# A fused channel-attention and SwiGLU kernel on one core: x's parts rounded in other steps, and a fourth pair's and a softmax's work placed elsewhere

## The chip, the cores and the metric

The kernel runs on one core of one Trainium2 chip. The metric is the device time of one execution in microseconds (us); lower is better. PE is TensorE (PEld its weight loads), DVE is VectorE, ACT is ScalarE, POOL is GpSimd, SP is SyncE, which here issues DMAs.

## The reference

```python
B, N, C, DFF = 2, 6016, 256, 1536
qn = q / (norm(q, axis=1) + 1e-6)           # over the N rows
kn = k / (norm(k, axis=1) + 1e-6)
s = kn.transpose(0, 2, 1) @ qn / tau        # C x C for each batch element
a = softmax(s)                              # exp(s - max), divided by its sum
x = (v @ a).reshape(B * N, C)               # 12032 rows
xn = x / sqrt(mean(x * x, -1) + 1e-6) * rms_g
g, val = xn @ w_gate, xn @ w_val
out = (silu(g) * val) @ w_out
```

## The kernel before

All matmuls run on operands split in a high and a low part: the high part is the value rounded to the matmul's type (a copy on ACT), the low part is the value minus its high part (a subtraction on POOL or DVE). Each product is then three matmuls, high by high, high by low and low by high.

A first phase reads q and k and builds batch element 0's attention. The rest runs over 24 blocks (`NB`) of up to 512 rows, block j = 0 to 23; blocks 0 to 11 (`B1` = 12) belong to batch element 0, the others to element 1. Every block is worked off in 12 steps f (`NF`), one per 128 columns of the hidden layer. Blocks 2 to 22 use a Strassen-like scheme for gate and value: `emit_step` emits seven products per step (each three matmuls) over three steps in flight. In one step PE does product 7 and 2 of the step two back (its sums are taken by DVE at L808 and L809), 3 and 6 of the step one back (ACT copies at L815), 5 and 1 of the new one (ACT copies at L820), then the output matmuls that are due, then product 4 of the oldest, which writes a PSUM buffer that DVE must have read at L808. Product 5 takes the PSUM buffer that was freed by the last reader of the step before: DVE at L836 after an odd step, ACT at L842 after an even one.

Two steps make one pair p of the hidden layer. In an odd step DVE multiplies gate and value (L827, L836) and ACT rounds the result (`gx`, `gy`, `gz` at L739) with POOL taking the low parts (L747). From block 4 on (`STRA`) the output product uses the seven-product scheme for pairs 1 to 4, which needs `run_turned` in the following even step on DVE: L726, L727 and L731. Its constants, sums of the weights `w_out`, are built by `build_so(k, piece)`: piece 0 sums on DVE (L659, L669), piece 1 rounds on ACT (L677), piece 2 takes low parts on DVE (L679). k = 3 is the fourth pair.

While block j goes through the steps, the next blocks are prepared by small pieces hung into its steps. The order of these pieces is written out by hand in tables: `steady` holds for j >= 5 and says what is emitted at the end of step f, `steady_mid` what is emitted inside step f, ahead of its output matmuls; `turn4` and `turn4_mid` are the tables of block 4. `at(j, f, ...)` adds single pieces at the end of step f of block j. Each engine works through its own instructions strictly in this order.

For block n = j + 1 the pieces are: the transposed rows `xnT` come back by 16 DMAs on SP's queue; ACT scales them (L558); POOL makes differences (`xp`, L570 and L575); then x is rounded in two rounds. Round 0 (`xh0` on ACT at L601 from `xnT`, `xl0` on POOL at L613) and round 1 (`xh1` on ACT at L601 from `xp`, two instructions of 128x512; `xl1`, two subtractions of 128x512 at L613) fill the buffers `xt` that block n's products read. For n = j + 2 there are the parts of v (`vh0`, `vl0`, `vh1`, `vl1`; L443 on ACT, L448 on POOL), x itself (L459 on PE), its squares (L475), its scaling (`n0`, `n1`; L500). Block 22 rounds its successor in another way and has no round 1. For j - 1 there are the output's sums (`copy` L1018, `sums_` L1028, `c0` and `c1` L1037) and the store (L1048).

`turn4` takes over step 1's `xh0` from `steady` and has `xh0` again in step 3. Batch element 1's softmax is spread over blocks 3 to 9: `softmax_exp` (L300, ACT) and `softmax_div` (L315 to L320, DVE: four instructions for each of the two halves, c = 0 and 1). Its result is first used for block 12, by the product x in step 3 of block 10.

Of the kernel before, what the change touches and what calls it, by code (L numbers as in the profile page):

```python
# [19 lines left out]
def kernel(  # L20
# [17 lines left out]
    nc = tc.nc  # L38
# [10 lines left out]
    STRA = 4  # L49
# [248 lines left out]
    def softmax_exp(b, c):  # L298
        z, mx = sm_t[b]
        nc.scalar.activation(  # L300
            out=z[:, c, :], in_=z[:, c, :], func=AF.Exp, scale=-1.0, bias=mx[:, c:c + 1],
            accum_out=mx[:, KC + c:KC + c + 1],
        )

    def softmax_div(b, c):
        if c == 0:
            a_hl[b] = []
            for i in range(2):
                a_hl[b].append(sm_p.tile([P, KC, C], F32R, tag=f"a{i}", name=f"a{i}_{b}"))
                if b == i == 0:  # L310
                    sm_p.tile([P, 8], F32, tag="apart", name="apart")
        ah, al = a_hl[b]
        z, mx = sm_t[b]
        s = mx[:, KC + c:KC + c + 1]
        nc.vector.tensor_scalar(out=s, in0=s, scalar1=1e-9, scalar2=None, op0=ALU.add)  # L315
        nc.vector.reciprocal(s, s)
        nc.vector.tensor_scalar(
            out=ah[:, c, :], in0=z[:, c, :], scalar1=s, scalar2=None, op0=ALU.mult
        )
        nc.vector.scalar_tensor_tensor(  # L320
            out=al[:, c, :], in0=z[:, c, :], scalar=s, in1=f32(ah[:, c, :]),
            op0=ALU.mult, op1=ALU.subtract,
        )
# [16 lines left out]
    B1 = NB // B  # L340
# [262 lines left out]
    def emit_xT_low(j, i, engine=nc.gpsimd):  # L603
        if j == NB - 1:
            if i == 0:
                engine.tensor_tensor(
                    out=xT[j][1], in0=moved[j][:, :, :blocks[j][2] * P], in1=f32(xT[j][0]),
                    op=ALU.subtract,
                )
            return  # L610
        src, hi, lo = xT_round(j, i)
        for o, x, y in zip(lo, src, hi):
            engine.tensor_tensor(out=o, in0=x, in1=f32(y), op=ALU.subtract)  # L613
# [41 lines left out]
    def build_so(k, piece):  # L655
        p = PAIRS[k]
        if piece == 0:
            t = s_tmp["so", k] = pool["wk"].tile([P, 4, 2 * P], F32, tag="wk", name=f"wo_{k}")
            nc.vector.tensor_tensor(  # L659
                out=t[:, :2], in0=f32(wo[0][:, 2 * p:2 * p + 2]), in1=f32(wo[1][:, 2 * p:2 * p + 2]),  # L660
                op=ALU.add,
            )
            a12, a22, a11, a21 = (t[:, i, e * P:(e + 1) * P] for i in range(2) for e in range(2))
            s1, s2, s3, s4 = (t[:, 2 + i, e * P:(e + 1) * P] for i in range(2) for e in range(2))
            for o, i0, i1, op in (
                (s1, a21, a22, ALU.add), (s2, s1, a11, ALU.subtract),
                (s3, a11, a21, ALU.subtract), (s4, a12, s2, ALU.subtract),
            ):
                nc.vector.tensor_tensor(out=o, in0=i0, in1=i1, op=op)  # L669
        else:  # L670
            t = s_tmp["so", k][:, 2:].rearrange("p i n -> p (i n)")
            src = (t[:, :3 * P], t[:, 3 * P:])
            hi, lo = (x[k] + [w[:, 2 * p + 1, P:]] for x, w in zip(so_hl, wo))
            if len(hi) > len(src):
                src = (t[:, :2 * P], t[:, 2 * P:3 * P], t[:, 3 * P:])
            for o, x in zip(hi, src) if piece == 1 else ():
                nc.scalar.activation(out=o, in_=x, func=AF.Copy)  # L677
            for o, x, y in zip(lo, src, hi) if piece == 2 else ():
                nc.vector.tensor_tensor(out=o, in0=x, in1=f32(y), op=ALU.subtract)  # L679
# [381 lines left out]
    with tc.manual_schedule():  # L1061
# [133 lines left out]
        def at(j, f, go):  # L1195
            extra.setdefault((j, f), []).append(go)
# [73 lines left out]
        at(STRA - 1, 6, new_so)  # L1270
        for i, k, f in ((0, 0, 10), (1, 0, 11), (2, 0, 12), (0, 1, 12), (1, 1, 13), (2, 1, 14), (0, 2, 14), (1, 2, 15)):
            at(STRA - 1 + f // NF, f % NF, lambda k=k, i=i: build_so(k, i))
        at(STRA, 7, last_so)
        for i in range(3):
            at(STRA, 9 + i, lambda i=i: build_so(3, i))

        at(3, 1, lambda: inverse_norms(1))
        at(3, 2, lambda: spread_norms(1, ps_m, "m"))
        at(3, 3, lambda: keep_norms(1))
        at(3, 5, lambda: softmax_min(1, 0))  # L1280
        at(3, 6, lambda: softmax_min(1, 1))
        at(7, 4, lambda: (softmax_exp(1, 0), softmax_exp(1, 1)))
        at(B1 - 3, 9, lambda: softmax_div(1, 0))
        at(B1 - 3, 11, lambda: softmax_div(1, 1))

        steps = [(j, f) for j in range(NB) for f in range(NF)]
        owed = []
# [30 lines left out]
        def of(m, go):  # L1318

            def run(j):  # L1320
                n = j + m
                if m < 0 and n < WINO or n >= NB:
                    return
                go(n)
            return run
# [11 lines left out]
        vh0, vl0, vh1, vl1 = (of(2, lambda n, go=go, h=h: go(n, h)) for h in range(2) for go in (split_v_high, split_v_low))  # L1337
        xh0, xl0, xh1, xl1 = (of(1, lambda n, go=go, i=i: go(n, i)) for i in range(2) for go in (emit_xT_high, emit_xT_low))

        steady = {  # L1340
            0: (vl0,),
            1: (xh0,),
            2: (copy, sums_),
            3: (vh1,),
            4: (xh1, c0, c1),
            5: (xl1, n0),
            6: (m0,),
            7: (load,),
            8: (m1,),
# [3 lines left out]
            1: (scale,),  # L1353
            2: (parts, v1),
            3: (xl0, x0),
            4: (vl1, q0, r0),
            5: (x1, q1, r1, store),
            6: (n1,),
            11: after(3, lambda n: split_v_high(n, 0)),
# [1 line left out]
        turn4 = {  # L1361
            **steady,
            0: (vh0, vl0),
            2: (),
            3: (xh0, v1),
            4: (vh1, c0, c1),
# [70 lines left out]
        for i, (j, f) in enumerate(steps):  # L1437
            outs = []
            owed.append((i + (2 if j < WINO else LAG + (j == NB - 1)), j, f))
            while owed and owed[0][0] <= i:  # L1440
                outs.append(owed.pop(0)[1:])
            k = min(j, 5)
            hooks = [
                [lambda go=go: go(j) for go in table[k].get(f, ())] for table in (pres, mids, ends)
            ]
            if j < WINO or j == NB - 1:
                if j == NB - 1 and f < 2:
                    low = []
                    emit_step(
                        None, None, i % 2, outs, mid=[lambda: low.append(emit_hidden(j, f, (), False))]  # L1450
                    )
                    low.pop()()
                    outs = []
                else:
                    if j == NB - 1 and f == 2:
                        run_later()
                    emit_hidden(j, f, weights.get((j, f), ()))
                for go in hooks[1]:
                    go()
                for o in outs:  # L1460
                    emit_all(o)
            else:
                if j == WINO and f < 2:
                    for o in outs:
                        emit_all(o)
                    outs = []
                emit_step(j, f, i % 2, outs, *hooks[:2])
                while late:
                    late.pop(0)()
            for go in hooks[2]:  # L1470
                go()
            for go in extra.get((j, f), []):
                go()
# [37 lines left out]
```

## Time and profile before

| | before |
|---|---|
| median of three runs | 1268.98 us (1267.22 to 1269.09) |
| profiled execution, its own time | 1268.32 us |
| its span, first to last instruction | 1266.5 us |
| mean granted TensorE clock | 0.999 |
| busy share PE / DVE / ACT / POOL | 99 / 79 / 68 / 53 % |

The span is that of the profiled execution; the 1.8 us between it and the execution's own time lie outside the first and the last instruction. A busy share is the time in which an engine had an instruction running. Matmuls overlap, so PE counts as busy through short gaps between them.

### The profile page before, as it was taken

How to read it: one execution, taken by the hardware profiler on the slowest of the kernel's cores; microseconds unless marked ns; L12 is line 12 of the kernel's file. 1: busy time of each engine (PE TensorE's matmuls, PEld its weight loads, DVE VectorE, ACT ScalarE, POOL GpSimd, SP SyncE). 2: the span in 40 equal slices, each digit the busy share in tenths (PEclk: the TensorE clock that was granted, in tenths of full speed). 3: DMA queues.
4: the chain of work that ended last, by engine and by line, in shares of the span. 5: the costliest groups of instructions: out<-in, count | busy, mean ns of one | idle time of the engine just before them, and what ended most of it. 6: DMA issues, size and time to landing. Idle time of an engine off the chain costs nothing.

```text
span 1266.5 us, 25188 instructions
## 1 busy us (share of the span) xinstructions
PE 1251.8 (99%) x9312; PEld 1198.9 (95%) x9312; DVE 1004.8 (79%) x1637; ACT 859.7 (68%) x1767; POOL 671.8 (53%) x564
## 2 busy tenths in 40 slices
PE   9999999999999999999999999999999999999998
PEld 8898989998999999999999999999999999999998
DVE  5789698666978878878879779779779779788773
ACT  5666547666677787777677677676777767777652
POOL 0120356574675566574675665665665765755430
PEclk9999999999999999999999999999999999999999
DMA  9868312020220211211202202202202202101211
GB/s 309 316 223 263 111 34 49 20 34 18 51 34 19 50 25 28 45 24 34 41 18 45 38 15 51 35 18 51 35 18 51 35 18 51 30 19 30 48 37 30
DMA packets 229371, 75.97 MB, mean 60 GB/s; under 512 B 186880, under 2 KB 220800, under 8 KB 229248
## 3 DMA queue, kind: packets, MB, share of 16 engines
q1 hardware_dynamic: 228416, 73.12, 24.3%
q8 instruction: 73, 1.20, 0.4%
q10 hardware_dynamic: 832, 1.25, 0.3%
q14 instruction: 50, 0.41, 0.1%
HBM read 48.50 MB, written 14.42 MB: 50 GB/s over the span
## 4 chain that ended last, share of the span: by engine, by line
PE 87%; DVE 4%; DMA 3%; ACT 2%; SPq 1%; issue 1%; POOL 1%; ACTq 0%; DVEq 0%; POOLq 0%
PE pu L779 39%; PE po L1003 23%; PE pq L779 6%; PE px L459 5%; PE s L185 5%; PE pg L896 3%; PE pv L896 3%; PE po L949 3%; DMA raw<-in_k_dram 2%; SPq L548 1%; SPq L353 0%; DVE gx L726 0%; DVE zg L808 0%; POOL gz L747 0%; DVE zg L727 0%
## 5 line engine op out<-in xcount | busy, mean ns | idle before, releaser
L779 PE MATMUL pu<-xt,w 128*128 128x256 f32 x2268 | 391.9, 281 | 1.6 <-DVE zg L808 1.3
L779 PE MATMUL pu<-xt,s 128*128 128x256 f32 x2268 | 355.5, 282 | 4.5 <-ACT t L815 2.8
L747 POOL TENSOR_TENSOR gy<-zg,gy 128x512 fp32r<-128x512 f32 x126 | 176.9, 1404 | 313.9 <-ACT gy L739 294.3
L779 PEld LDWEIGHTS pu<-xt,w 128*128 128x128 f32 x2268 | 326.5, 188 | 13.0 <-DVE zg L808 2.1
L779 PEld LDWEIGHTS pu<-xt,s 128*128 128x128 f32 x2268 | 311.7, 189 | 17.0 <-DVE zg L836 3.6
L820 ACT ACTIVATE t<-pu 128x512 f32<-128x512 f32 x252 | 151.5, 601 | 105.6 <-DVE zv L809 55.0
L1003 PE MATMUL po<-gx,w 128*128 128x256 f32 (+1 forms) x984 | 190.6, 314 | 0.0
L827 DVE TENSOR_TENSOR zg<-zg,zv 128x768 f32<-128x768 f32 x126 | 169.2, 1343 | 11.3 <-DVE zv L809 0.5
L739 ACT ACTIVATE gx<-zg 128x768 fp32r<-128x768 f32 (+1 forms) x126 | 95.7, 760 | 113.9 <-DVE zg L836 65.9
L1003 PEld LDWEIGHTS po<-gx,w 128*128 128x128 f32 x984 | 140.9, 189 | 4.7
L779 PE MATMUL pq<-xt,w 128*128 128x256 f32 x756 | 130.0, 280 | 0.0
L815 ACT ACTIVATE t<-pu 128x256 f32<-128x256 f32 x252 | 95.5, 379 | 45.0 <-PE pu L779 44.7
L808 DVE TENSOR_TENSOR zg<-pu,t 128x512 f32<-128x512 f32 x126 | 86.1, 683 | 41.2 <-PE pu L779 23.8
L747 POOL TENSOR_TENSOR gz<-zg,gz 128x512 fp32r<-128x512 f32 x76 | 116.4, 1532 | 0.0
L779 PEld LDWEIGHTS pq<-xt,w 128*128 128x128 f32 x756 | 107.0, 189 | 0.0
L824 ACT ACTIVATE zg<-zg 128x768 f32<-128x768 f32 x126 | 105.6, 838 | 0.0
L808 DVE TENSOR_TENSOR zv<-pu,t 128x512 f32<-128x512 f32 x126 | 84.6, 672 | 16.4 <-ACT zg L842 7.6
L185 PE MATMUL s<-raw 128*128 128x256 f32 x376 | 85.9, 382 | 3.7 <-DMA raw<-in_k_dram 3.7
L747 POOL TENSOR_TENSOR gx<-zg,gx 128x512 fp32r<-128x512 f32 x50 | 65.2, 1304 | 41.1 <-ACT gx L739 40.9
L1003 PE MATMUL po<-gy,w 128*128 128x512 f32 x300 | 85.4, 393 | 0.0
L185 PEld LDWEIGHTS s<-raw 128*128 128x128 f32 x376 | 70.2, 191 | 14.4 <-DMA raw<-in_k_dram 3.2
L739 ACT ACTIVATE gy<-zg 128x512 fp32r<-128x512 f32 x126 | 79.9, 634 | 1.4 <-PE po L1003 1.1
(173 smaller groups left out, 2317.4 us busy)
## 6 DMA issues: line engine op xcount, KB each, us to landing
v<-in_v_dram SPq DMA_DIRECT2D x84, 128.0 KB, 3.7
xnT<-xw SPq DMA_DIRECT2D x336, 32.0 KB, 1.9
out_dram<-ob SPq DMA_DIRECT2D x84, 128.0 KB, 3.3
raw<-in_q_dram SPq DMA_DIRECT2D x20, 512.0 KB, 4.9
raw<-in_k_dram SPq DMA_DIRECT2D x19, 512.0 KB, 5.7
wraw<-in_moe_w_gate_dram SPq DMA_DIRECT2D x12, 256.0 KB, 5.7
wraw<-in_moe_w_val_dram SPq DMA_DIRECT2D x12, 256.0 KB, 6.4
wraw<-in_moe_w_out_dram SPq DMA_DIRECT2D x12, 256.0 KB, 6.5
```

The costliest lines, as they stand in the source:

```text
L185: nc.tensor.matmul(out=s_ps[b][:, c, :], lhsT=r[:, 1, t, c * P:(c + 1) * P], rhs=r[:, 0, t, :], start=(t0 + t == 0 and c == 0), stop=(t0 + ...
L459: nc.tensor.matmul(out=px[:, i, :], lhsT=w[:, c, i * P:(i + 1) * P], rhs=x[:, c, :], start=(i == 0 and c == 0 and m == 0), stop=(c == KC - ...
L739: nc.scalar.activation(out=gh, in_=hh, func=AF.Copy)
L747: engine.tensor_tensor(out=gl, in0=hh, in1=f32(gh), op=ALU.subtract)
L779: nc.tensor.matmul(out=out, lhsT=wm[wi], rhs=xm[xi], start=(start and q == 0), stop=(q == 2), skip_group_check=True,)
L808: nc.vector.tensor_tensor(out=z[:, 1:], in0=u, in1=t[:, :2], op=ALU.add)
L815: nc.scalar.activation(out=mt[:, 0], in_=mu[:, 1], func=AF.Copy)
L820: nc.scalar.activation(out=nt[:, 1:], in_=nu, func=AF.Copy)
L824: nc.scalar.activation(out=zg[:, 1:], in_=zg[:, 1:], func=AF.Silu)
L827: nc.vector.tensor_tensor(out=zg[:, 1:], in0=zg[:, 1:], in1=z, op=ALU.mult)
L896: nc.tensor.matmul(out=t[:, :n], lhsT=wgv[wi][:, f, c, wj, :], rhs=x[xi][:, c, :n], start=(m == 0), stop=(m == 3 * KC - 1),)
L1003: nc.tensor.matmul(out=acc[b][:, o:o + g.shape[-1]], lhsT=w, rhs=g, start=first, stop=True, skip_group_check=True,)
```

## The change

Four things change, and all are places in the order; the arithmetic stays, but for one thing that was done twice.

- In blocks 5 to 22 `xh1` moves from the end of step 4 to the end of step 3, behind `vh1`. `xl1` moves from POOL at the end of step 5 to DVE inside step 4 (`xl1v`).
- In block 4 the first of the two `xh0` is taken out.
- The fourth pair's constants are built in steps 5, 6 and 9 of block 4, not in steps 9, 10 and 11.
- The two halves of `softmax_exp` are done after step 8 of block 7 and after step 8 of block 8, not both after step 4 of block 7. The two halves of `softmax_div` are done after step 1 and inside step 2 of block 10, not after steps 9 and 11 of block 9.

```diff
--- before.py
+++ after.py
@@ -1270,18 +1270,19 @@
         at(STRA - 1, 6, new_so)
         for i, k, f in ((0, 0, 10), (1, 0, 11), (2, 0, 12), (0, 1, 12), (1, 1, 13), (2, 1, 14), (0, 2, 14), (1, 2, 15)):
             at(STRA - 1 + f // NF, f % NF, lambda k=k, i=i: build_so(k, i))
-        at(STRA, 7, last_so)
-        for i in range(3):
-            at(STRA, 9 + i, lambda i=i: build_so(3, i))
+        at(STRA, 5, last_so)
+        for i, f in enumerate((5, 6, 9)):
+            at(STRA, f, lambda i=i: build_so(3, i))

         at(3, 1, lambda: inverse_norms(1))
         at(3, 2, lambda: spread_norms(1, ps_m, "m"))
         at(3, 3, lambda: keep_norms(1))
         at(3, 5, lambda: softmax_min(1, 0))
         at(3, 6, lambda: softmax_min(1, 1))
-        at(7, 4, lambda: (softmax_exp(1, 0), softmax_exp(1, 1)))
-        at(B1 - 3, 9, lambda: softmax_div(1, 0))
-        at(B1 - 3, 11, lambda: softmax_div(1, 1))
+        at(7, 8, lambda: softmax_exp(1, 0))
+        at(8, 8, lambda: softmax_exp(1, 1))
+        at(B1 - 2, 1, lambda: softmax_div(1, 0))
+        mid_extra = {(B1 - 2, 2): lambda: softmax_div(1, 1)}

         steps = [(j, f) for j in range(NB) for f in range(NF)]
         owed = []
@@ -1337,13 +1338,15 @@
         vh0, vl0, vh1, vl1 = (of(2, lambda n, go=go, h=h: go(n, h)) for h in range(2) for go in (split_v_high, split_v_low))
         xh0, xl0, xh1, xl1 = (of(1, lambda n, go=go, i=i: go(n, i)) for i in range(2) for go in (emit_xT_high, emit_xT_low))

+        xl1v = of(1, lambda n: emit_xT_low(n, 1, nc.vector))
+
         steady = {
             0: (vl0,),
             1: (xh0,),
             2: (copy, sums_),
-            3: (vh1,),
-            4: (xh1, c0, c1),
-            5: (xl1, n0),
+            3: (vh1, xh1),
+            4: (c0, c1),
+            5: (n0,),
             6: (m0,),
             7: (load,),
             8: (m1,),
@@ -1353,7 +1356,7 @@
             1: (scale,),
             2: (parts, v1),
             3: (xl0, x0),
-            4: (vl1, q0, r0),
+            4: (vl1, xl1v, q0, r0),
             5: (x1, q1, r1, store),
             6: (n1,),
             11: after(3, lambda n: split_v_high(n, 0)),
@@ -1361,6 +1364,7 @@
         turn4 = {
             **steady,
             0: (vh0, vl0),
+            1: (),
             2: (),
             3: (xh0, v1),
             4: (vh1, c0, c1),
@@ -1464,6 +1468,7 @@
                     for o in outs:
                         emit_all(o)
                     outs = []
+                hooks[1].extend([mid_extra[j, f]] if (j, f) in mid_extra else [])
                 emit_step(j, f, i % 2, outs, *hooks[:2])
                 while late:
                     late.pop(0)()
```

The next rows are ACT's order in block 4, from the end of step 1 on. `xt0_5` is the high part of x of block 5, `xnT_5` its source, `so0` and `wo_1` the constants of the output product; `t_4_1` is L815's copy that PE waits for. Before:

```order
L739 ACTIVATE gx0_3_10_3236<-zg_3_10_3160 128x512
L601 ACTIVATE xt0_5_3245<-xnT_5_3132 128x256
L601 ACTIVATE xt0_5_3245<-xnT_5_3132 128x512
L677 ACTIVATE so0_2851<-wo_1_3194 128x384
L677 ACTIVATE w0_103<-wo_1_3194 128x128
L815 ACTIVATE t_4_1_3201<-pu_4_1_3200 128x256
L820 ACTIVATE t_4_2_3252<-pu_4_2_3251 128x512
```

and after the change:

```order
L739 ACTIVATE gx0_3_10_3236<-zg_3_10_3160 128x512
L677 ACTIVATE so0_2851<-wo_1_3194 128x384
L677 ACTIVATE w0_103<-wo_1_3194 128x128
L815 ACTIVATE t_4_1_3201<-pu_4_1_3200 128x256
L820 ACTIVATE t_4_2_3248<-pu_4_2_3247 128x512
```

The two rows at L601 are gone, and nothing stands between the rounding of `gx0_3_10` and the constants.

The next rows are DVE's order in step 4 of block 15, as in blocks 5 to 21; `os_14` are the output sums of block 14, `zg_15_2` and `zv_15_3` the sums of two products. Before:

```order
L808 TENSOR_TENSOR zg_15_2_10817<-pu_15_2_10689,t_15_2_10690 128x512
L809 TENSOR_TENSOR zg_15_2_10817<-pq_15_2_10813,t_15_2_10690 128x256
L1037 TENSOR_TENSOR os_14_10739<-po0_14_10239,os_14_10739 128x512
L1037 TENSOR_TENSOR os_14_10739<-po1_14_10242,os_14_10739 128x512
L808 TENSOR_TENSOR zv_15_3_10868<-pu_15_3_10745,t_15_3_10746 128x512
```

and after the change:

```order
L808 TENSOR_TENSOR zg_15_2_10815<-pu_15_2_10685,t_15_2_10686 128x512
L809 TENSOR_TENSOR zg_15_2_10815<-pq_15_2_10811,t_15_2_10686 128x256
L613 TENSOR_TENSOR xt1_16_10682<-xp_16_10712,xt0_16_10681 128x512 x2
L1037 TENSOR_TENSOR os_14_10735<-po0_14_10237,os_14_10735 128x512
L1037 TENSOR_TENSOR os_14_10735<-po1_14_10240,os_14_10735 128x512
L808 TENSOR_TENSOR zv_15_3_10866<-pu_15_3_10741,t_15_3_10742 128x512
```

The two subtractions at L613 stand between L809 and the output sums at L1037. On POOL they stood at the end of step 5, between the small operations of `rr_17_1` and the subtraction for `gy1_15_3`, as in the next rows, which are POOL's order of before:

```order
L747 TENSOR_TENSOR gy1_15_1_10799<-zg_15_0_10698,gy0_15_1_10798 128x512
L484 TENSOR_SCALAR ss_17_1_10899<-ss_17_1_10899 128x2
L488 TENSOR_TENSOR rr_17_1_10903<-ss_17_1_10899,mhalf_100 128x2
L613 TENSOR_TENSOR xt1_16_10686<-xp_16_10716,xt0_16_10685 128x512 x2
L747 TENSOR_TENSOR gy1_15_3_10924<-zg_15_2_10817,gy0_15_3_10923 128x512
```

After the change these five rows are the same without the one at L613.

The next rows are ACT's order in block 7 around the first half of `softmax_exp` after the change; `z_1` is batch element 1's softmax, and step 9 begins with the rounding of `gy0_7_5`:

```order
L842 ACTIVATE zg_7_6_5646<-pu_7_6_5535 128x256
L300 ACT_TABLE_LOAD
L300 ACTIVATE z_1_1402,mx_1_1403<-z_1_1402,mx_1_1403 128x256
L739 ACTIVATE gy0_7_5_5623<-zg_7_4_5544 128x512
L739 ACTIVATE gz0_7_5_5625<-zg_7_4_5544 128x512
L815 ACTIVATE t_7_8_5638<-pu_7_8_5637 128x256
L820 ACTIVATE t_7_9_5705<-pu_7_9_5704 128x512
L739 ACTIVATE gx0_7_6_5744<-zg_7_6_5646 128x768
L815 ACTIVATE t_7_9_5705<-pu_7_9_5704 128x256
L820 ACTIVATE t_7_10_5756<-pu_7_10_5755 128x512
L824 ACT_TABLE_LOAD
L824 ACTIVATE zg_7_8_5764<-zg_7_8_5764 128x768
```

Before, both halves stood behind one table load, between `xh1` and the rounding of `gy0_7_1`, with the second load at L824 two steps on. Now the same two loads stand around each half, once in block 7 and once in block 8.

## Rows read from the trace of the kernel before

**Rows 1.** The page, first section: busy us (share of span) xinstructions.

```profile
PE 1251.8 (99%) x9312; PEld 1198.9 (95%) x9312; DVE 1004.8 (79%) x1637; ACT 859.7 (68%) x1767; POOL 671.8 (53%) x564
```

**Rows 2.** Waits of PE: who waited <- releaser: us in total, times, longest.

```profile
PE pu L779 <- ACT t L815: 2.8, 1, 2.8
PE pu L779 <- DVE zg L808: 1.3, 3, 0.5
...
PE pu L779 <- ACT zg L842: 1.0, 1, 1.0
PE pu L779 <- DVE zg L836: 0.5, 1, 0.5
```

**Rows 3.** Timeline, block 15, steps 5 to 8: start us, us, engine, line, tiles.

```profile
857.72 3.32 POOL L613 TENSOR_TENSOR xt<-xp,xt 128x512 fp32r<-128x512 f32 x2
...
859.92 1.67 DVE L727 TENSOR_TENSOR zg<-zg 128x512 f32<-128x512 f32 x1
...
862.27 0.87 PE L779 MATMUL pu<-xt,s 128*128 128x256 f32 x6
...
863.19 0.65 DVE L808 TENSOR_TENSOR zv<-pu,t 128x512 f32<-128x512 f32 x1
...
863.90 1.30 POOL L747 TENSOR_TENSOR gz<-zg,gz 128x512 fp32r<-128x512 f32 x1
863.91 0.61 PE L779 MATMUL pu<-xt,w 128*128 128x256 f32 x3
864.21 1.81 DVE L827 TENSOR_TENSOR zg<-zg,zv 128x768 f32<-128x768 f32 x1
...
865.88 1.14 PE L779 MATMUL pu<-xt,s 128*128 128x256 f32 x6
```

**Rows 4.** Timeline of PE, block 20, step 8.

```profile
1107.76 1.13 PE L779 MATMUL pu<-xt,s 128*128 128x256 f32 x6
```

**Rows 5.** By line and shape, whole span: busy us, mean ns, idle before.

```profile
L727 DVE TENSOR_TENSOR zg<-zg 128x512 f32<-128x512 f32 x76 | 67.3, 886 | 2.6
...
L650 DVE TENSOR_TENSOR s<-wk,s 128x512 fp32r<-128x512 f32 x6 | 4.2, 708 | 0.0
```

**Rows 6.** Timeline, block 15, steps 2 to 5: [idle time before, what ended it].

```profile
843.56 1.67 DVE L1028 TENSOR_TENSOR os<-po,os 128x256 f32<-128x256 f32 x4 [2.14 <-ACT os L1018]
...
849.82 0.39 ACT L815 ACTIVATE t<-pu 128x256 f32<-128x256 f32 x1 [0.67 <-PE pu L779]
849.96 1.29 POOL L448 TENSOR_TENSOR vt<-vw,vt 128x512 fp32r<-128x512 f32 x1
...
852.04 1.29 DVE L1037 TENSOR_TENSOR os<-po,os 128x512 f32<-128x512 f32 x2 [2.15 <-PE po L1003]
...
856.30 0.51 PE L779 MATMUL pu<-xt,w 128*128 128x256 f32 x3
```

**Rows 7.** Timeline of ACT, block 4, end of step 1.

```profile
303.05 0.63 ACT L601 ACTIVATE xt<-xnT 128x512 fp32r<-128x512 f32 x1 [4.58 <-DMA xnT<-xw]
```

**Rows 8.** Windows of PE, block 4: stretch, length, busy (matmuls), granted clock.

```profile
304.60:308.40 3.80, 3.79 (x19) 0.56 0.00 0
308.40:312.20 3.80, 3.80 (x28) 0.99 0.02 4
```

**Rows 9.** Windows of tile wo, block 4, after steps 9, 11: DVE busy.

```profile
336.00:338.50 2.50, 1.67 (x5) 0.00 (x0) 1.00 0.21 55
345.00:347.60 2.60, 1.56 (x3) 0.00 (x0) 1.00 0.03 7
```

**Rows 10.** Timeline of ACT, block 7, steps 4 and 5.

```profile
464.52 1.28 ACT L300 ACT_TABLE_LOAD   x1
465.82 0.51 ACT L300 ACTIVATE z<-z,mx 128x256 f32<-128x256 f32 x1
```

**Rows 11.** Windows of ACT, block 7, steps 8 to 10: length, busy.

```profile
480.00:486.00 6.00, 3.57 (x7) 1.00 0.08 22
```

**Rows 12.** Windows of tile mx, block 9, after step 9: DVE busy.

```profile
578.00:584.00 6.00, 1.15 (x4) 0.00 (x0) 1.00 0.13 34
```

## The prediction

> **What bounds the kernel now.** I read the page first: PE is busy 99% of the span [rows 1]. So only time in which PE stands still, or runs at its lower clock, can be won, and no engine that is taken off DVE, ACT or POOL counts by itself. Next I read who ends PE's waits [rows 2]. In the Strassen blocks there are six: one long wait for ACT at L815, and short ones for DVE at L808 and L836 and for ACT at L842. I looked up each in the timeline. The 2.8 us lie in block 4, step 2; of the three L808 waits two lie in block 4 (steps 10 and 11) and one in block 9 (step 11); L842's lies in block 7, step 7; L836's in block 4, at its very end.
>
> A wait costs more than its row says. A matmul of 256 columns is drawn with some 0.27 us, and the next one follows 0.12 us after it: six take 0.87 and three 0.51 [rows 3, 6], which is 0.12 us for each further one. So idle time is counted only from 0.15 us after the due start, and the first matmul after a wait is followed about 0.1 us late. I add 0.25 us for each listed wait. For the same reason delays under 0.15 us make no wait at all, and they are seen only in the length of a group. Block 15 shows them: product 4 of step 7 takes 0.61 us instead of 0.51, and six matmuls in step 8 take 1.14 instead of 0.87 [rows 3, 6]. That is 0.37 us in a block, and block 20 reads the same [rows 4]. All of blocks 5 to 21 have this work, 17 blocks.
>
> **The change part by part.**
>
> *The double round in block 4.* ACT's L601 at the end of step 1 waits 4.58 us for the DMAs that bring `xnT` [rows 7]; L815 stands behind it, and PE behind L815, 2.8 us [rows 2], with the addition 3.1. After it the granted clock falls: in the next 3.80 us it is 0.56 on average, so mostly at the lower of its two levels (1.2 GHz), and PE does 19 matmuls where the following 3.80 us hold 28 [rows 8]. By the count that costs 9/28 of 3.80, 1.2 us; by the clock 0.44 of 3.80, 1.7 us; I take 1.4. Taking the round out removes both: 4.5 us (4.3 to 4.8). The second `xh0` two steps later now comes as much earlier. L601 went on at 303.05, and its own place, two steps of some 4 us behind step 1, is later than that without PE's stop too, so I cost a new wait there at nothing.
>
> *Round 1's low parts from POOL to DVE, blocks 5 to 21.* POOL's two subtractions run from 857.72 to 861.04. DVE's L727, which starts at 859.92 and reads and writes SBUF alone as they do, takes 1.67 us [rows 3]. Over the span it takes 0.89 on average [rows 5]; with 17 of the 76 at 1.67 the other 59 come to (67.3 - 28.4)/59 = 0.66. So DVE loses 1.0 us just ahead of L808 of step 7, which starts only at 863.19 though PE's product 7 was done before the matmuls drawn at 862.27 began [rows 3]; product 4 (863.91) waits for L808, and L827 then starts so late that POOL's `gz`, from 863.90 on, is ahead of it: 1.81 us instead of about 0.95, and L836 behind it is late for product 5, the long group at 865.88. With POOL free at 859.92, DVE is up to 1.0 us earlier at L808, and L827 can start before `gz` does. I expect both delays to go: 17 x 0.37 = 6.3, taken as 6.2 (1.7 to 6.3: only the first, 0.10 each, or both).
>
> Its price: two subtractions on DVE, 0.71 us each by the nearest form [rows 5], 1.4 together, held up by POOL's L448 for at most its 1.29 [rows 6]: 1.4 to 2.7 us. They stand where DVE waits 2.15 us for PE ahead of L1037 [rows 6]. At the upper end L1037 is 0.6 us late. Next in line is L808 of step 5, some 0.7 us of work right behind L1037: without the delay it ends near 854, and product 4 of that step starts at 856.30 [rows 6], so 2 us are left. I cost it at nothing. `xh1` on ACT (two of some 0.6 us) fills an idle 0.67 ahead of L815 and makes it 0.5 us late, until about 850.7; product 7 of step 5, which needs it, comes behind the output matmuls for which L1037 waits until 852.04 [rows 6]. Nothing either.
>
> *The exponentials.* Now they cost PE 1.0 + 0.25 less the 0.37 counted above, 0.9 us, in block 7. After the change each half brings two table loads of 1.28, 0.51 for itself [rows 10] and about 0.2 for reading its sum, 3.3 us in all. In the 6 us of block 7 where the first half will stand, ACT is idle 2.4 us [rows 11]. Hidden wholly, each costs nothing; else 0.9, what does not fit. L815 and L842 have some room in these steps, so I take 0.2 each and a gain of 0.5 (-0.9 to 0.9).
>
> The Trainium skill ("ScalarE: Activation LUTs", "Table sets: the hidden batching unit") says to batch activations by table set, and in "What ACT_TABLE_LOAD costs" it puts each switch at 1283 ns plus a drain of about 1380 ns. This speaks against splitting the two halves. The trace agrees with the load and shows no drain: the exponential starts at 465.82, 0.02 us after the load [rows 10]. An estimate by that page: a half would take about 6.0 us, 3.6 more than the idle time; both would cost 7.2 and not 0.4, and the sum below would be 6.0 and not 12.8.
>
> *The quotients.* One half is four instructions, 1.15 us of DVE [rows 12]. After steps 9 and 11 DVE has no room: one listed wait of 0.4 + 0.25, and smaller delays beside it; I take 1.0 (0.6 to 1.2). In the new places DVE waits 2.14 us ahead of L1028 [rows 6], enough for the second half; the first delays L808 of step 2, which has room as in step 5. The use in step 3 of block 10 is behind both. Gain 0.9 (0.5 to 1.2).
>
> *The fourth pair.* In block 4 DVE's 1.67 us after step 9 and 1.56 after step 11 [rows 9] are what the two L808 waits and L836's come from: 0.9 + 0.5 + 0.75 = 2.2 us, up to 2.5 with delays too short to be listed. Steps 6 to 11 have the extra work of `run_turned`, so DVE has little room anywhere there. The first piece moves to the end of step 5, where it is followed by POOL's `xl1`, which in block 4 stays on POOL; the last moves to step 9. I expect 1.5 us of stall to remain (0.6 to 3.2), spread over steps 7 to 11. Gain 0.7 (-1.0 to 1.6).
>
> Sum: 4.5 + 6.2 + 0.5 + 0.9 + 0.7 = 12.8 us. The profiled execution would go from 1268.32 to 1255.5, the median of 1268.98 to 1256.2; the runs lie on both sides of the profiled one, and I forecast 1255.8. Where every stall named goes wholly the sum is 4.8 + 6.3 + 0.9 + 1.2 + 1.6 = 14.8, 1253.5.
>
> **The rivals.**
>
> *The second steady delay stays* (chance 0.13). L827 is still held until `gz` ends, since `gz` comes from ACT, whose order in step 6 does not change. Then L836 is as late as now, and 17 x 0.27 = 4.6 us are not won: 1260.4. For it speaks L827's 1.81; against it that L827 would start up to 0.7 us earlier, ahead of `gz`.
>
> *The small moves cost what they gain* (0.12). Both halves of the exponential pay 0.9, and block 4 keeps 2.5 or more: 12.8 - 1.4 - 1.0 = 10.4, 1258.2. For it speaks that DVE is full in steps 6 to 11 and that the loads double; against it ACT's idle 2.4 us. The batching rule of "ScalarE: Activation LUTs" in the Trainium skill stands on this rival's side.
>
> *The wait for the DMAs only moves* (0.05): `xh0` or the scaling at L558 in step 3 would wait for the same transfer, PE stops there, and 4.5 us are not won: 1260.3. Against it: the transfer was over at 303.05.
>
> *Slower* (0.05): the two subtractions make DVE the bound in steps 4 and 5. It decides when they take over 2.15 + 2 = 4.2 us, by being held at each of them by a whole POOL subtraction, and by more POOL work that comes earlier behind L448. Each further microsecond then costs 17 us: with 5.2 us the time is 1255.8 + 17 = 1273, slower than before. Against it: only L448 is near (1.29), which gives 2.7. The Trainium skill ("SBUF — State Buffer", "Who interferes with whom") says that whichever of DVE and GpSimd issues first on their shared port pair holds it for the whole instruction and the other blocks. The trace agrees (L727's 1.67 for 0.66), and by it the moved work is blocked too, only where DVE has idle time.
>
> **How the numbers follow.** My forecast has 0.65, with a range of its own of 1253.3 to 1258.5. For 8 in 10 I add the cases near 1258 and 1260: 1252.8 to 1260.3, the low end a little under the full sum for the scatter of runs. About 0.2%, 2.5 us, is what a measurement of this kernel can tell from no change. All cases but the last are faster by more: 0.95. The last one is split: 0.02 within, 0.03 slower.
>
> **What the profile of the changed kernel would show.** L613 with `xp` on DVE 34 times, near 0.7 to 1.4 us each; L727's mean near 0.7; groups of 0.51 and 0.87 us in steps 7 and 8 of blocks 5 to 21; no wait of PE for L815 near 300 us, no stretch at the lower clock in block 4, and the mean granted clock 1.000; two more table loads; no wait for L808 in block 9. I am wrong if L836 still ends late in step 8, if L1037's delay reaches product 4 of step 5, or if block 4 keeps its waits at L808.

## The result

The changed kernel takes 1257.34 us, the median of 6 runs (1255.54 to 1258.23); beside them the kernel before took 1268.78 (1267.22 to 1269.09). The ratio is 0.9909 with a 95% interval of 0.9896 to 0.9921, so 10 to 13 us are won. The forecast was 1255.8, with 1252.8 to 1260.3 as the range. The profiled execution took 1255.54, its span 1253.8.

In the page of the kernel after, this line answers to [rows 1]:

```profile
PE 1245.6 (99%) x9312; PEld 1196.5 (95%) x9312; DVE 1021.6 (81%) x1671; ACT 864.2 (69%) x1767; POOL 627.5 (50%) x530
```

PE still fills 99% of the span, of a span that is 12.7 us shorter: matmuls that were drawn long in the steady blocks, or at the lower clock in block 4, are short now. The waits of PE, against [rows 2]:

```profile
engine line waited for: us in total, times, longest us
PE pu L779 <- ACT zg L842: 1.9, 3, 0.7
...
PE s L185 <- DMA raw<-in_k_dram: 0.9, 2, 0.6
...
```

The waits for L815, L808 and L836 are gone. Left in the Strassen blocks are three for L842: one in block 4 (0.44), and two of 0.72 where the exponentials now stand, in blocks 7 and 8. The line of `s` belongs to the start, before the blocks. It read 3.7 us before and 0.9 here, and between 0.9 and 4.6 in the profiles of this study, with no edit near it. So the two profiles differ by some 1.7 us for a reason that is not the change's (the first L820 starts at 199.42 before and at 197.70 after), and I compare by blocks.

For that I took from the trace, for each matmul, the time from its start to the next one's start, less the median of its form, and added up what exceeds 0.05 us. This counts the short delays too that make no wait. PE's stall, in us:

| kernel | block 4 | 5, 6, 11 to 21, each | 7 | 8 | 9 | 10 | blocks 4 to 21 |
|---|---|---|---|---|---|---|---|
| before | 7.14 | 0.31 to 0.67 | 1.34 | 0.35 | 1.51 | 0.36 | 15.7 |
| after | 1.71 | 0 | 1.32 | 1.32 | 0 | 0.06 | 4.4 |

The difference, 11.3 us, is that of the medians, 11.4. Of the 4.4 us that are left, 2.6 lie in the two blocks with the exponentials.

**Steady blocks.** Rows from steps 4 to 8 of block 15, picked from the timeline of the kernel after, against [rows 3, 6]:

```profile
start us, us, engine line op out<-in xcount [idle before <-releaser]
839.49 2.46 DVE L613 TENSOR_TENSOR xt<-xp,xt 128x512 fp32r<-128x512 f32 x2
839.66 1.74 POOL L448 TENSOR_TENSOR vt<-vw,vt 128x512 fp32r<-128x512 f32 x1
841.87 1.27 DVE L1037 TENSOR_TENSOR os<-po,os 128x512 f32<-128x512 f32 x2
843.07 0.68 DVE L808 TENSOR_TENSOR zv<-pu,t 128x512 f32<-128x512 f32 x1
...
849.61 0.69 DVE L727 TENSOR_TENSOR zg<-zg 128x512 f32<-128x512 f32 x1
...
852.66 0.51 PE L779 MATMUL pu<-xt,w 128*128 128x256 f32 x3
853.15 1.29 DVE L827 TENSOR_TENSOR zg<-zg,zv 128x768 f32<-128x768 f32 x1
853.58 2.02 POOL L747 TENSOR_TENSOR gz<-zg,gz 128x512 fp32r<-128x512 f32 x1
855.48 0.87 PE L779 MATMUL pu<-xt,s 128*128 128x256 f32 x6
855.63 0.69 DVE L808 TENSOR_TENSOR zg<-pu,t 128x512 f32<-128x512 f32 x1 [0.86 <-POOL gz L747]
```

The two subtractions take 2.46 us on DVE, held by L448, and L448 is held by them. They fill the time in which DVE waited 2.15 us before L1037, and L808 of step 5 is not late. L727 takes 0.69 in place of 1.67. Now L827 starts ahead of `gz`, and POOL is the one that is held (2.02). PE's groups are at their usual 0.51 and 0.87. The last row is one to keep in mind: L808 of an even step waits here 0.86 us for POOL's `gz`, although nothing is late.

**Block 4** around step 2, the two stretches of [rows 8] in the kernel after:

```profile
core 0: us, PE busy (x) PEld busy (x) DVE busy (x) ACT busy (x) POOL busy (x), PEclk, DMA share, GB/s
304.60:308.40 3.80, 3.80 (x32) 3.66 (x31) 2.68 (x4) 2.92 (x7) 3.65 (x3) 1.00 0.02 4
308.40:312.20 3.80, 3.80 (x29) 3.54 (x28) 2.47 (x4) 3.49 (x9) 3.73 (x4) 1.00 0.00 0
```

PE runs through at the full 2.4 GHz, where before it stood still and then went on at 0.56 of it.

**Block 7**, from the end of step 8, in the kernel after: what the first half of the exponential does (rows picked from the timeline).

```profile
471.10 0.37 ACT L842 ACTIVATE zg<-pu 128x256 f32<-128x256 f32 x1
471.49 1.28 ACT L300 ACT_TABLE_LOAD   x1
472.78 0.51 ACT L300 ACTIVATE z<-z,mx 128x256 f32<-128x256 f32 x1
473.29 0.62 ACT L739 ACTIVATE gy<-zg 128x512 fp32r<-128x512 f32 x1
474.04 1.94 POOL L747 TENSOR_TENSOR gy<-zg,gy 128x512 fp32r<-128x512 f32 x1 [5.37 <-ACT gy L739]
475.94 1.28 POOL L747 TENSOR_TENSOR gz<-zg,gz 128x512 fp32r<-128x512 f32 x1
477.26 0.69 DVE L808 TENSOR_TENSOR zg<-pu,t 128x512 f32<-128x512 f32 x1 [2.10 <-PE pu L779]
478.01 0.63 PE L779 MATMUL pu<-xt,w 128*128 128x256 f32 x3
478.40 0.60 ACT L820 ACTIVATE t<-pu 128x512 f32<-128x512 f32 x1 [1.46 <-DVE zg L809]
479.01 1.28 ACT L824 ACT_TABLE_LOAD   x1
...
481.06 0.37 ACT L842 ACTIVATE zg<-pu 128x256 f32<-128x256 f32 x1
481.48 0.62 PE L779 MATMUL pu<-xt,s 128*128 128x256 f32 x3 [0.72 <-ACT zg L842]
```

The load and the exponential stand directly ahead of ACT's rounding of `gy`, which starts 1.8 us later than L842's end would let it. POOL's `gy`, held by L827 for 0.65 us more, and `gz` follow, until 477.22. DVE's L808 of step 10 starts at 477.26. Its wait is labelled with PE, but `gz` ended 0.04 us ahead, the trace has POOL's semaphore as the last raised (477.24) of those that this L808 waits for, and in block 15 the same wait is POOL's; `zg` has two buffers, and `gz` of the pair two back reads the one that L808 writes. So product 4 is late (0.33), and L820 waits 1.46 for L809. Only then can the second load begin. It makes both Silu activations late, and PE waits for L842 (0.99). That is 1.32 us, and block 8 shows the same.

### The profile page after: what moved, and what is told of

Read it like the earlier page. It is cut to its first block, busy times and chain, and to the rows that moved or that the text cites. A ratio compares the mean times of both kernels' runs of the same rounds, so it can differ in the third digit from the quotient of the medians.

```text
span 1253.8 us, 25167 instructions
## 1 busy us (share of the span) xinstructions
PE 1245.6 (99%) x9312; PEld 1196.5 (95%) x9312; DVE 1021.6 (81%) x1671; ACT 864.2 (69%) x1767; POOL 627.5 (50%) x530
## 4 chain that ended last, share of the span: by engine, by line
PE 97%; DMA 1%; DVE 1%; ACT 1%; POOL 0%; issue 0%; SPq 0%; DVEq 0%; ACTq 0%; POOLq 0%
PE pu L779 42%; PE po L1003 26%; PE pq L779 7%; PE s L185 6%; PE px L459 5%; PE pg L896 3%; PE pv L896 3%; PE po L949 3%; DMA raw<-in_k_dram 1%; PE warm_first L1087 0%; POOL gz L747 0%; DVE zg L808 0%; ACT L824 0%; PE pn L228 0%; ACT zg L824 0%
## 5 line engine op out<-in xcount | busy, mean ns | idle before, releaser
L779 PE MATMUL pu<-xt,s 128*128 128x256 f32 x2268 | 351.6, 281 | 1.9 <-ACT zg L842 1.9
L747 POOL TENSOR_TENSOR gy<-zg,gy 128x512 fp32r<-128x512 f32 x126 | 168.6, 1338 | 330.1 <-ACT gy L739 305.3
L779 PEld LDWEIGHTS pu<-xt,s 128*128 128x128 f32 x2268 | 310.5, 189 | 11.5 <-ACT zg L842 2.7
L820 ACT ACTIVATE t<-pu 128x512 f32<-128x512 f32 x252 | 151.1, 600 | 104.1 <-PE pu L779 45.9
L827 DVE TENSOR_TENSOR zg<-zg,zv 128x768 f32<-128x768 f32 x126 | 167.1, 1326 | 10.6
L808 DVE TENSOR_TENSOR zg<-pu,t 128x512 f32<-128x512 f32 x126 | 86.5, 686 | 58.4 <-PE pu L779 28.9
L747 POOL TENSOR_TENSOR gz<-zg,gz 128x512 fp32r<-128x512 f32 x76 | 130.2, 1713 | 0.0
L815 ACT ACTIVATE t<-pu 128x256 f32<-128x256 f32 x252 | 95.9, 380 | 46.8 <-PE pu L779 45.6
L824 ACT ACTIVATE zg<-zg 128x768 f32<-128x768 f32 x126 | 105.5, 838 | 0.0
L808 DVE TENSOR_TENSOR zv<-pu,t 128x512 f32<-128x512 f32 x126 | 84.5, 670 | 16.9 <-ACT zg L842 7.6
```

The costliest lines, as they stand in the source:

```text
L747: engine.tensor_tensor(out=gl, in0=hh, in1=f32(gh), op=ALU.subtract)
L779: nc.tensor.matmul(out=out, lhsT=wm[wi], rhs=xm[xi], start=(start and q == 0), stop=(q == 2), skip_group_check=True,)
L808: nc.vector.tensor_tensor(out=z[:, 1:], in0=u, in1=t[:, :2], op=ALU.add)
L815: nc.scalar.activation(out=mt[:, 0], in_=mu[:, 1], func=AF.Copy)
L820: nc.scalar.activation(out=nt[:, 1:], in_=nu, func=AF.Copy)
L824: nc.scalar.activation(out=zg[:, 1:], in_=zg[:, 1:], func=AF.Silu)
```

## The experiments

Each kernel was timed beside the kernel before on the same chip. The stall by blocks is read as in the table above. Of the timelines, rows are picked.

**One part at a time, applied to the kernel before.**

*The doubled round of x.*

```diff
         turn4 = {
...
             0: (vh0, vl0),
+            1: (),
             2: (),
```

> The kernel before with only the doubled round of x in block 4 taken out. If the DMA wait and its low-clock stretch near 300 us go for good: 4.5 us shorter than before, about 1264.3 (block 4 falls from 56.15 us to about 51.6). Rival, the wait only moves to a later step: 0 to 1 us shorter, about 1268.

Measured: 1262.93 against 1268.12, ratio 0.9960 (0.9946 to 0.9974). Block 4 goes from 56.15 to 51.53 us and its stall from 7.14 to 2.53; the other blocks keep theirs within 0.05. The part is worth 4.6 us, as the first theory had it: the wait didn't move.

*x's second half sooner, low part on VectorE.*

```diff
-            3: (vh1,),
-            4: (xh1, c0, c1),
-            5: (xl1, n0),
+            3: (vh1, xh1),
+            4: (c0, c1),
+            5: (n0,),
...
-            4: (vl1, q0, r0),
+            4: (vl1, xl1v, q0, r0),
```

> The kernel before with only x's second half rounded a step sooner and its low part on VectorE. If the 0.37 us a block of steps 7 and 8 (17 blocks) is the whole of this part: 6.2 us shorter, about 1262.6, and no idle time of TensorE in steps 7 and 8 of blocks 11 to 18. Rival, the second delay (the POOL rounding of the last z group) stays: 1.7 us shorter, about 1267.1.

Measured: 1261.52, ratio 0.9955 (0.9940 to 0.9970). Blocks 5, 6, 8 and 10 to 21 have no stall at all, and blocks 7 and 9 lose some 0.3 and 0.5 of theirs: 6.4 to 6.6 us by blocks. The rival falls.

*The exponentials.*

```diff
-        at(7, 4, lambda: (softmax_exp(1, 0), softmax_exp(1, 1)))
+        at(7, 8, lambda: softmax_exp(1, 0))
+        at(8, 8, lambda: softmax_exp(1, 1))
```

> The kernel before with only the fourth exponentials (batch element 1) moved, from step 4 of block 7 to step 8 of blocks 7 and 8. By the prediction: 0.5 us shorter, about 1268.3. By what the profile of the changed kernel shows (VectorE's product of step 10 waits for a buffer of zg that POOL frees 2 us late, in both blocks): 1.3 us for each half, less the 0.9 saved in step 4, so about 1.7 us longer than before, 1270.5.

Measured: 1270.43, ratio 1.0025 (1.0014 to 1.0035). Alone, this part makes the kernel 2.3 us slower. Blocks 7 and 8 stall for 1.78 and 2.08 us, together 3.86, where they had 1.34 and 0.35. The prediction's reading falls.

*The fourth pair's sums.*

```diff
-        at(STRA, 7, last_so)
-        for i in range(3):
-            at(STRA, 9 + i, lambda i=i: build_so(3, i))
+        at(STRA, 5, last_so)
+        for i, f in enumerate((5, 6, 9)):
+            at(STRA, f, lambda i=i: build_so(3, i))
```

> The kernel before with only the fourth pair's sums moved to steps 5, 6 and 9 of block 4 (the doubled round is still in). By the prediction: 2.2 to 2.5 us of stalls become 1.5, so 0.7 shorter, about 1268.1. Rival, the sums depend on what the round of x leaves free and are no cheaper there than before: 0 to 1 us longer.

Measured: 1267.32, ratio 0.9997 (0.9987 to 1.0006), which can't be told from no change. The trace can tell: behind step 9 block 4 stalled for 2.49 us before, and here for 1.69 behind step 6.

*The quotients.*

```diff
-        at(B1 - 3, 9, lambda: softmax_div(1, 0))
-        at(B1 - 3, 11, lambda: softmax_div(1, 1))
+        at(B1 - 2, 1, lambda: softmax_div(1, 0))
+        mid_extra = {(B1 - 2, 2): lambda: softmax_div(1, 1)}
```

> The kernel before with only the quotients of batch element 1 moved from steps 9 and 11 of block 9 into steps 1 and 2 of block 10. By the prediction: block 9's late stalls (0.07, 0.32 and 0.78 us) go, 0.9 shorter with what block 10 keeps, about 1267.3. Rival, the quotients find VectorE as full in block 10 and pay the same there: no change, 1268.2.

Measured: 1267.48 against 1268.43, ratio 0.9993 (0.9983 to 1.0003). Block 9 falls from 1.51 us of stall to 0.36, what every steady block of the kernel before has; block 10 keeps its 0.36. So 1.15 us by the trace, and the rival falls.

By their medians the five parts come to 5.2 + 6.6 - 2.3 + 0.8 + 0.95 = 11.3 us, the whole change to 11.4. They add up, but not closely: by the ratios they come to 8.9 against 11.5, and each of the five is uncertain by 1.2 to 1.9 us. The stalls say it better. Over blocks 4 to 21 the five kernels stall for 4.7, 6.6, -2.0, 0.8 and 1.15 us less than the kernel before, 11.2 together, and the changed kernel for 11.3 less.

**Why the exponentials cost 1.3 us each.** Three kernels built from the changed one. The first puts each half inside step 9, behind the roundings of `gy` and `gz`:

```diff
-        at(7, 8, lambda: softmax_exp(1, 0))
-        at(8, 8, lambda: softmax_exp(1, 1))
...
+        mid_extra |= {(7, 9): lambda: softmax_exp(1, 0), (8, 9): lambda: softmax_exp(1, 1)}
```

> The changed kernel with each half of the fourth exponentials issued inside step 9 of blocks 7 and 8, behind the roundings of gy and gz of that step. If the 1.3 us a half come from gy and gz being rounded 2 us late (POOL then frees zg's buffer late and VectorE's product of step 10 waits): nearly all of it goes, 2.0 to 2.6 us shorter than the changed kernel, about 1255.0. Rival, the table loads and the exponentials just don't fit into ScalarE's idle time of two steps, wherever they stand: the same 1.3 a half, about 1257.3.

Measured: 1255.92 against 1268.75, ratio 0.9898 (0.9883 to 0.9913). Blocks 7 and 8 stall for 0.23 us each. Block 7 of this kernel in the timeline:

```profile
476.78 1.29 POOL L747 TENSOR_TENSOR gz<-zg,gz 128x512 fp32r<-128x512 f32 x1
...
477.88 1.28 ACT L300 ACT_TABLE_LOAD   x1
...
479.14 0.67 DVE L808 TENSOR_TENSOR zg<-pu,t 128x512 f32<-128x512 f32 x1
...
481.33 1.28 ACT L824 ACT_TABLE_LOAD   x1
...
483.32 1.09 PE L779 MATMUL pu<-xt,s 128*128 128x256 f32 x6
```

The same two loads now cost next to nothing: `gz` is done at 478.07, a microsecond ahead of L808, and the second load makes one group of six 0.22 us longer. The place costs, not the work.

The second puts both halves, with one pair of loads, where a `gy` follows but no `gz`, which this kernel has only from block 4 on:

```diff
-        at(7, 8, lambda: softmax_exp(1, 0))
-        at(8, 8, lambda: softmax_exp(1, 1))
+        at(3, 8, lambda: (softmax_exp(1, 0), softmax_exp(1, 1)))
```

> The changed kernel with both halves of the fourth exponentials at the end of step 8 of block 3, where no gy and gz of a round are rounded. Buffer theory: the 2.64 us of blocks 7 and 8 go and none comes back in block 3 (49.60 us now), about 1254.7. Rival, two exponentials and two table loads hold ScalarE too long in any block: 0.7 to 1.3 us come back in block 3, about 1255.7.

Measured: 1255.32, ratio 0.9894 (0.9879 to 0.9909), the lowest of the medians, 2 us below the changed kernel's, though the two intervals overlap. Blocks 7 and 8 have no stall; block 3 gets 0.28 us more, behind the Silu of step 10 (its timeline):

```profile
282.02 1.29 POOL L747 TENSOR_TENSOR gy<-zg,gy 128x512 fp32r<-128x512 f32 x1 [0.18 <-ACT gy L739]
...
284.15 0.69 DVE L808 TENSOR_TENSOR zg<-pu,t 128x512 f32<-128x512 f32 x1 [1.01 <-PE pq L779]
...
286.12 1.28 ACT L824 ACT_TABLE_LOAD   x1
...
288.06 1.15 PE L779 MATMUL pu<-xt,s 128*128 128x256 f32 x6
288.17 0.36 ACT L842 ACTIVATE zg<-pu 128x256 f32<-128x256 f32 x1
```

Here the exponentials stand ahead of `gy` too. But POOL has one subtraction to do and not two, it ends at 283.31, and L808 at 284.15 does not wait for it. So the rival's 0.7 to 1.3 does not come. The third leaves the places as the changed kernel has them and takes the loads away. With Silu in place of the exponential it leaves out batch element 1's softmax:

```diff
-            out=z[:, c, :], in_=z[:, c, :], func=AF.Exp, scale=-1.0, bias=mx[:, c:c + 1],
+            out=z[:, c, :], in_=z[:, c, :], func=AF.Silu if b else AF.Exp, scale=-1.0, bias=mx[:, c:c + 1],
```

> The changed kernel with the Silu function in place of the exponential for batch element 1, which changes what the kernel computes, so that ScalarE does the same two activations at the same two places with no table load. If the two loads of 1.28 us around each half are what makes gy and gz late and then the next Silu late: blocks 7 and 8 keep less than 0.3 us of their 1.32 each, about 1254.8. Rival, the activations with their accumulators and the place at the end of step 8 are enough for it: 0.5 us or more stays in each block, about 1256.2.

One run gave 1253.77, and blocks 7 and 8 keep 0.10 us each. Block 7:

```profile
472.03 0.51 ACT L300 ACTIVATE z<-z,mx 128x256 f32<-128x256 f32 x1
...
472.52 0.62 ACT L739 ACTIVATE gy<-zg 128x512 fp32r<-128x512 f32 x1
...
474.53 1.29 POOL L747 TENSOR_TENSOR gz<-zg,gz 128x512 fp32r<-128x512 f32 x1
```

An activation and its accumulator ahead of `gy` are borne, so it is the loads that don't fit in that place. Both are taken away here, so the first is not priced apart from the second. A third buffer of `zg` would test the buffer by itself; no kernel here has one.

**Does x's low part have to leave POOL, or only come sooner?** Two kernels, each with half of that part.

```diff
-            4: (vl1, xl1v, q0, r0),
+            4: (vl1, xl1, q0, r0),
```

> The changed kernel with x's second low part on POOL as before, but still issued a step sooner. If VectorE is needed for it: the 0.37 us of steps 7 and 8 come back in up to 17 blocks, up to 6.3 us longer than the changed kernel, about 1263.6. Rival, the sooner step is what takes the delay away: no longer than the changed kernel, 1257.3.

```diff
-            5: (n0,),
+            5: (xl1v, n0),
...
-            4: (vl1, xl1v, q0, r0),
+            4: (vl1, q0, r0),
```

> The changed kernel with x's second low part on VectorE, but issued at the end of step 5, where POOL's copy of it stood before. If taking it off POOL is enough: 1257.3, no idle time in steps 7 and 8. Rival, VectorE then has 1.7 us more to do just ahead of the products of step 6, and they come late by 0.2 to 1.0 us a block: 3.4 to 17 us longer than the changed kernel.

Measured: 1257.71 (ratio 0.9912, 0.9897 to 0.9926) with POOL, a step sooner; 1258.41 (0.9921, 0.9904 to 0.9937) with VectorE, a step later. With POOL the steady blocks have no stall either; POOL works on it from 841.77 to 844.3, long before L727:

```profile
841.77 2.55 POOL L613 TENSOR_TENSOR xt<-xp,xt 128x512 fp32r<-128x512 f32 x2
842.61 1.29 DVE L1037 TENSOR_TENSOR os<-po,os 128x512 f32<-128x512 f32 x2 [2.15 <-PE po L1003]
...
850.48 0.69 DVE L727 TENSOR_TENSOR zg<-zg 128x512 f32<-128x512 f32 x1
```

With VectorE in step 5 the two subtractions take 1.27 us, and the rival's 0.2 to 1.0 us a block don't come. Only blocks 11 and 21 stall, 0.36 and 0.57 us, and block 11 shows the second delay that was a rival in the prediction:

```profile
662.89 1.30 POOL L747 TENSOR_TENSOR gz<-zg,gz 128x512 fp32r<-128x512 f32 x1
662.96 2.04 DVE L827 TENSOR_TENSOR zg<-zg,zv 128x768 f32<-128x768 f32 x1
...
664.93 0.41 DVE L836 TENSOR_TENSOR zg<-pu,zg 128x256 f32<-128x256 f32 x1
```

`gz` starts 0.07 us ahead of L827 and holds it until 664.2. Either half of the part removes the collision with L727, and with that nearly all of the 6.4 us; the sooner step alone is as good as both.

**Can block 4's remaining 1.7 us be had as well?** The largest part of its stall in the kernel after, 0.71 us behind step 6, comes from this (timeline of block 4, steps 5 and 6):

```profile
313.43 1.51 DVE L659 TENSOR_TENSOR wo<-w,w 128x512 f32<-128x512 f32 x1
...
314.97 1.02 DVE L669 TENSOR_TENSOR wo<-wo 128x128 f32<-128x128 f32 x4
...
315.82 3.31 POOL L613 TENSOR_TENSOR xt<-xp,xt 128x512 fp32r<-128x512 f32 x2
315.91 0.68 DVE L808 TENSOR_TENSOR zg<-pu,t 128x512 f32<-128x512 f32 x1
...
317.04 0.60 ACT L820 ACTIVATE t<-pu 128x512 f32<-128x512 f32 x1 [1.29 <-DVE zg L809]
...
318.00 1.67 DVE L727 TENSOR_TENSOR zg<-zg 128x512 f32<-128x512 f32 x1
...
319.70 0.41 ACT L842 ACTIVATE zg<-pu 128x256 f32<-128x256 f32 x1
```

The sums hold L808, L820 waits for L809, and L842 comes late to PE. The sums do something else too: block 4's `xl1` is still on POOL (315.82 to 319.13), and L727, made late by the sums, now runs into it and takes 1.67 us. Before, this L727 started at 321.81, ahead of `xl1` at 322.33, and took 0.69. So the move brings the steady blocks' collision into block 4. What that has of the 1.0 us behind steps 7 to 11 no run here separates. The experiment takes the kernel with the exponentials in block 3, and cuts piece 0 in two (`part` picks its instructions):

```diff
-        for i, f in enumerate((5, 6, 9)):
-            at(STRA, f, lambda i=i: build_so(3, i))
+        for i, f, part in ((0, 5, (0,)), (0, 7, (1, 2)), (1, 9, ())):
+            at(STRA, f, lambda i=i, part=part: build_so(3, i, part))
...
-        mid_extra = {(B1 - 2, 2): lambda: softmax_div(1, 1)}
+        mid_extra = {(B1 - 2, 2): lambda: softmax_div(1, 1), (STRA + 1, 0): lambda: build_so(3, 2)}
```

> The changed kernel with both halves of the fourth exponentials at the end of step 8 of block 3, and the fourth pair's sums cut smaller: its first sum on VectorE at the end of step 5 of block 4 alone, the other four at the end of step 7, the roundings of high parts on ScalarE at the end of step 9, the low parts inside step 0 of block 5. If block 4's 1.7 us come from 2.5 us of sums standing in one piece ahead of VectorE's products of step 6: 0.5 to 0.8 us stay there, about 1254.4. Rival, VectorE is as full in steps 7 to 11 and the pieces pay the same where they now stand: 1.7 us stay, 1255.3.

Measured: 1256.83 against 1268.43, ratio 0.9905 (0.9890 to 0.9920). Block 4 keeps 1.90 us, and block 5 gets 1.92 that it didn't have. Even the rival was too kind. L727 of block 4 (L731 there) still takes 1.67 in this kernel. Step 0 of block 5 (there L808 of the other kernels is L812, L679 is L683):

```profile
344.78 1.54 DVE L683 TENSOR_TENSOR so_iq<-wo,so_dg 128x256 fp32r<-128x256 f32 x1
...
346.25 1.36 DVE L683 TENSOR_TENSOR so_ones<-wo,so_ident 128x128 fp32r<-128x128 f32 x1
...
347.73 0.68 DVE L812 TENSOR_TENSOR zv<-pu,t 128x512 f32<-128x512 f32 x1
...
348.46 0.62 PE L783 MATMUL pu<-xt,w 128*128 128x256 f32 x3 [1.65 <-DVE zv L812]
```

Two small subtractions take 2.9 us there, while POOL does `gy` and `gz` beside them; the same two took 0.69 (0.41 and 0.28) at the end of step 9 of block 4 in the kernel after. Behind step 7, where the four sums now stand, block 4 stalls for 0.99, against 0.33 in the kernel after. Where in blocks 4 and 5 these sums would cost nothing, if anywhere, stays open.

## Why the prediction was right, and which term was wrong

The terms as forecast, and what the blocks give for each within the whole change:

| term | forecast gain, us | measured, us | read from |
|---|---|---|---|
| double round | 4.5 | 4.65 | block 4, steps 2 and 3: 4.65 to 0 |
| low parts on DVE | 6.2 | 6.4 | steps 7 and 8 of blocks 5 to 21, to 0 |
| exponentials | 0.5 | -1.6 | 1.01 (block 7 without the steady part) to 2.64 |
| quotients | 0.9 | 1.1 | 1.51 - 0.35 in block 9, to 0.06 in block 10 |
| fourth pair | 0.7 | 0.8 | 2.49 to 1.71 in block 4 |
| sum | 12.8 | 11.3 | |

*The double round* went as predicted, by its steps: no wait at L815 near 300 us, no stretch at the lower clock, no wait further on.

*The low parts.* Cause and size were right: POOL's subtractions held L727, and the two delays behind it went together because L827 now comes ahead of `gz`. The price was 2.46 us of the 1.4 to 2.7 named, and DVE's idle time before L1037 covered it. The prediction put the cure down to the engine; the runs show that the sooner step does it alone. One reading was off: the prediction took L727 as held in all 17 blocks, which left 0.66 us for the other instances. In the trace of the kernel before 15 take 1.67 and the other 61 take 0.69; in blocks 14 and 18 POOL holds L726 in its place (1.91 and 1.79 us). The hold is 1.0 us all the same, so the term did not suffer.

*The exponentials* are the term that failed. The step was "L815 and L842 have some room in these steps, so I take 0.2 each". It added up 3.3 us of ACT work against 2.4 us of idle time, as if only the total had to fit, and looked for who waits at L815 and L842 alone. The work stood ahead of `gy`. What it made late was POOL, then the buffer of `zg`, then L808, and with L820 the second load. Inside step 9 the same 3.3 us cost 0.23. The range given for this term, -0.9 to 0.9, didn't reach to -1.6 either, since its lower end was two halves at the old price of 0.9 and not a new wait.

The rule to gather activations by table set (the Trainium skill, "ScalarE: Activation LUTs", "Table sets: the hidden batching unit") gave the right sign: by splitting, the same exponentials went from 1.01 to 2.64 us, and gathered again in block 3 they cost 0.28. The drain of about 1380 ns (the Trainium skill, "ScalarE: Activation LUTs", "What ACT_TABLE_LOAD costs") isn't seen in the kernel after: after both loads of block 7 the next activation starts within 0.02 us. And the estimate of 7.2 us for both halves that was worked out from it is far above 2.64. What cost is where the load stands more than how many there are: two pairs of loads in a good place cost 0.46, one pair in the old place 1.01.

*The quotients and the fourth pair* came out within 0.2 us of their terms. The rest of block 4 lies in steps 7 to 11, as forecast.

Of the rivals, "the small moves cost what they gain" came nearest: 1258.2 against 1257.34. Half of it happened, the exponentials'; block 4 did not keep its 2.5. Of the signs, L613 with `xp` is on DVE 34 times, L727's mean is 0.705, ACT has two more table loads, and the mean granted clock is 1.000, all as said. Only L613's times, 0.76 to 1.78 us each, go beyond the 1.4 named.

## What to carry to other kernels

When work is moved into an engine's idle time, a sum of idle time over a stretch says little: take the first instruction behind the new place, follow who reads it, and go on until a buffer comes free, since the wait may turn up two engines further. Work with a fixed extra, like a table load, belongs behind the roundings and evictions that others wait for, not ahead of them, unless whoever waits has time to spare, as POOL had in block 3. And price the parts of a change by stalls per block from the trace: parts worth under a microsecond, which whole runs could not tell from nothing, could be read there, and they added up to the measured whole.

## What the runs showed of the hardware

DVE and POOL held each other in both directions, and a small instruction could be held for several times its length. L683's 128x128 subtraction took 1.36 us with POOL's `gy` and `gz` beside it, and 0.28 right after. L448 on POOL took 1.74 beside L613 on DVE, and 1.29 in the same block of the kernel that leaves this work to POOL. L808, which reads PSUM, took 0.65 to 0.69 in all 252 instances of the kernel after, beside POOL's work too. Which of the two is held can turn on 0.07 us: with `xl1` on VectorE at the end of step 5, `gz` started 0.07 and 0.06 us ahead of L827 in blocks 11 and 21, which stalled, and 0.15 us or more behind it in the other 15, which did not.
